# Attention and two MLPs on one core: integer turns and q's second order on ScalarE, the first pair turned on TensorE

## The chip, the cores and the metric

The kernel runs on one core of one Trainium2 chip. The metric is the device time of one execution in microseconds (us); lower is better. The five engines are named as in the profile: PE (TensorE; PEld is its weight load), DVE (VectorE), ACT (ScalarE), POOL (GpSimd) and SP (SyncE, which here only issues DMAs; SPq is its queue).

## What is computed

```python
# q, k, v: (4 batches, 8 heads, 1152 rows, 64), float32
q_pool = q.reshape(B, H, S // 2, 2, D).mean(axis=3)          # 576 query rows
scores = (1 / sqrt(D)) * q_pool @ k.T                         # 576 x 1152 per head
attn = softmax(scores)
x = (attn @ v) -> reshaped to (2304, 512)
h = x @ w_in;    g = h * cos(h);      y = g @ w_out           # 512 -> 2048 -> 512
h2 = y @ w_in2;  g2 = h2 * sigmoid(h2); out = g2 @ w_out2     # 512 -> 2048 -> 512
```

The weights of both MLPs are float64 in memory; the output is (2304, 512) float32. float32 factors are carried as two float16 numbers, a high and a low part, and multiplied on PE as such.

## The kernel before

**Attention.** The heads are handled in 16 pairs (two heads of one batch). A pair has nine tiles of 128 query rows (the ninth holds the last 64 rows of both heads). For each pair `pair_loads` issues the loads of q, k and v on SP's queue, and `pair_prep` prepares them: GpSimd adds the two rows that are averaged, VectorE takes absolute maxima, a small matmul spreads them and three VectorE operations make the scales; then q and k are split into a high and a low float16 part (ScalarE writes the high part, VectorE the low one), and a DMA transpose turns each. q stands twice in the buffer `qn`: once as (high, low) and once as (low, high), so that two matmuls with the same k, which is (high, low), give all cross products. The copy in the other order costs a second ScalarE operation (L509 runs twice) and a VectorE copy (L513), and the transpose of q (L515) has 18 blocks of 128 x 128, as many as that of k (L525).

A tile then goes through a chain: PE makes 128 x 1152 scores (L549, L557) in two PSUM tiles `sp`; VectorE scales them into `sc` and takes the extreme (L568, then `nb` at L573); ScalarE takes the exponential (L576) and the high float16 part (`hl`, L582); GpSimd subtracts to get the low part (L150, three operations); a DMA transpose on SP's queue turns both parts (`hlT`, L589, 18 blocks); PE multiplies with v (L600, L604). PE does the last step of a tile four tiles after its first (`LAG = 4`), and there are four buffers each of `sc`, `hl` and `hlT`.

**First MLP.** While the first batch's four pairs run, the float64 weights are loaded and split (`layer1_weight_steps`). From the second batch on, units of the first MLP are put between the tiles (`share`, `layer1`): nine blocks of 256 tokens, each with 16 slices `f` of the hidden dimension. `g1_unit` makes a slice (12 matmuls, L685) in one half of a PSUM tile `hp` (tag `h`, two buffers); at each odd `f`, `g1_evac` brings two slices to `hk` in SBUF (L701), scaled to turns of h over 2 pi. Four slices make a group, 36 groups in all. `g_cos_begin` rounds the group's turns to whole numbers with the constant MAGIC (L713) and subtracts (L714); `g_cos_end` takes the sine (L720), multiplies by h (L723), makes the high part `gh` (L728) and, on GpSimd, the low part `gl` (L150). The work tile `tt` has two buffers (`NB_TT = 2`), which the finished output `y32` of a block (L749, stored by L752) uses as well. `g2_unit1` is the second product (L740).

**Second MLP.** Behind the last tile of attention the rest of the first MLP runs with the preparation of the second one's weights (`layer2_weight_steps`, L343 to L374), then the second MLP (L685 again, L854).

**Order.** A scheduler orders the instructions of each engine by priorities over a simulated timeline, and waits for a free buffer where a tag has none; `pin` (`tc.keep_in_program_order`) keeps an instruction in the order of the program. So a change in one place shifts the order in others. Each engine and each DMA queue executes its own list in order.

Of the kernel before, what the change touches and what calls it, by code (L numbers as in the profile page):

```python
# [18 lines left out]
DRAM = bass.MemoryType.DRAM  # L19

EXP_MASK = 0x7F800000
MAGIC = 12582912.0
# [5 lines left out]
NB_N, NB_SC, NB_H, NB_T, NB_S = 2, 4, 4, 4, 5  # L28
LOW_HL, LOW_G, LOW_W = 3, 2, 2
X_LAG = 40  # L30
W1_BUFS, WT_BUFS = 3, 3
# [8 lines left out]
NB_HK, NB_TT, NB_G, SIN_N = 2, 2, 2, 2  # L40
# [9 lines left out]
def attention_moe_moe_kernel(ctx, tc, q, k, v, w_in1, w_out1, w_in2, w_out2, out):  # L50
# [3 lines left out]
    nc = tc.nc  # L54
    B, H, S, D = q.shape
# [4 lines left out]
    KC = S // 128  # L60
# [12 lines left out]
    mean = const.tile([128, 128], F32, name="mean")  # L73
    halfpi = const.tile([128, 1], F32, name="halfpi")
    floor3 = const.tile([128, 1], F32, name="floor3")

    def make_consts():
        nc.vector.memset(mean, 2.0**-7)
        nc.vector.memset(halfpi, math.pi / 2)
        nc.vector.memset(floor3, 2.0**-14 - 0.5)  # L80

    GW = 256

# [97 lines left out]
    def layer1_weight_steps(w, srcs, stage, pspool, eng, bufs, wt_bufs, period, offs, first):  # L181
# [71 lines left out]
        for i, x in enumerate(pieces):  # L253
            g = []
            if i < first:
                g.append(piece_steps(*x, lambda ins: ins))
# [179 lines left out]
    def pair_new(at, b, j):  # L436

        P = Pair()  # L440
        P.b, P.j = b, j
        P.on_pool = PREP_POOL if b == 0 else 0
        P.q = at.src.tile([128, 2 * NT + 1, 2, D], F32, tag="stq", name="stq", bufs=1)
        P.k, P.v = (
            [at.src.tile([128, KC, D], F32, tag="stg", name="st" + nm, bufs=NB_S) for i in range(2)] for nm in "kv"
        )
        return P

    def pair_loads(P):
        heads = (P.j, P.j + NP)  # L450
        n = NT * 128 * 2
        for i, h in enumerate(heads):
            nc.sync.dma_start(
                out=P.q[:, i * NT:(i + 1) * NT], in_=q[P.b, h, 0:n, :].rearrange("(p t r) d -> p t r d", t=NT, r=2)
            )
            nc.sync.dma_start(
                out=P.q[i * 64:(i + 1) * 64, 2 * NT], in_=q[P.b, h, n:, :].rearrange("(p r) d -> p r d", r=2)
            )
            yield
        for src, t in ((k, P.k), (v, P.v)):  # L460
            for i, h in enumerate(heads):
                nc.sync.dma_start(out=t[i], in_=src[P.b, h].rearrange("(p c) d -> p c d", c=KC))
                yield

    def split(hi, lo, src, s, on_pool):
        nc.scalar.activation(out=hi, in_=src, func=AF.Copy, scale=s)
        if on_pool:
            nc.scalar.activation(out=src, in_=src, func=AF.Copy, scale=s)
            nc.gpsimd.tensor_tensor(out=lo, in0=src, in1=hi, op=ALU.subtract)
        else:  # L470
            nc.vector.scalar_tensor_tensor(out=lo, in0=src, scalar=s, in1=hi, op0=ALU.mult, op1=ALU.subtract)

    def pair_prep(at, P):
        NQ = 2 * NT + 1
        qs = P.q[:, :, 0, :]
        nc.gpsimd.tensor_tensor(out=qs, in0=qs, in1=P.q[:, :, 1, :], op=ALU.add)
        m = small.tile([128, 5], F32, name="pm", tag="pm")
        for i in range(2):
# [12 lines left out]
        s = small.tile([128, 3], F32, name="ps_", tag="ps_", bufs=3)  # L491
        u = small.tile([128, 3], F32, name="pu_", tag="pu_", bufs=3)
        yield from early(scale_steps(m3, ps_h, (s, u), 12), P_CH)
        P.s = s
        P.su = small.tile([128, 1], F32, name="psu", tag="psu", bufs=3)
        nc.vector.tensor_scalar(
            out=P.su, in0=u[:, 0:1], scalar1=u[:, 1:2], scalar2=-0.125 / math.sqrt(D), op0=ALU.mult, op1=ALU.mult
        )
        P.vt = [None] * 2

        def do_v(i):

            P.vt[i] = vt = at.vt[(2 * (P.b * NP + P.j) + i) % VT_BUFS]
            split(vt[:, :, 0, 0:D], vt[:, :, 1, 0:D], P.v[i], s[:, 2:3], P.on_pool >= 2)


        qn = at.src.tile([128, 2, NQ, 2, D], F16, tag="kn", name="qn", bufs=NB_N)
        for e in range(2):
            nc.scalar.activation(out=qn[:, e, :, e, :], in_=qs, func=AF.Copy, scale=s[:, 0:1])  # L509
        nc.vector.scalar_tensor_tensor(  # L510
            out=qn[:, 0, :, 1, :], in0=qs, scalar=s[:, 0:1], in1=qn[:, 0, :, 0, :], op0=ALU.mult, op1=ALU.subtract
        )
        nc.vector.tensor_copy(qn[:, 1, :, 0, :], qn[:, 0, :, 1, :])  # L513
        qT = at.p.tile([128, 2, NQ, 128], F16, tag="qT", name="qT", bufs=2)
        nc.sync.dma_start_transpose(  # L515
            out=qT.rearrange("p e n k -> p (e n) k"), in_=qn.rearrange("p e n s d -> p (e n s d)")
        )
        P.qT = [qT[:, e] for e in range(2)]
        yield
        kn = at.src.tile([128, 2, KC, 2, D], F16, tag="kn", name="kn", bufs=NB_N)  # L520
# [4 lines left out]
        nc.sync.dma_start_transpose(  # L525
            out=kT.rearrange("p i c k -> p (i c) k"), in_=kn.rearrange("p i c s d -> p (i c s d)")
        )
        P.kT = [kT[:, i].rearrange("p c k -> p (c k)") for i in range(2)]
        yield
        for i in range(2):  # L530
            do_v(i)
            yield

    segs = [(o, min(512, S - o)) for o in range(0, S, 512)]

# [168 lines left out]

    def g_cos_begin(mp, blk):
# [175 lines left out]
    if True:  # L881
# [6 lines left out]
        at = att_pools(att_stack)  # L888
# [161 lines left out]
        for n, (b, j) in enumerate(pairs):  # L1050
# [7 lines left out]
            for o in range(0, len(seq), GT):  # L1058
                G = Pair()
# [211 lines left out]
```

## Time and profile before

| | |
|---|---|
| time, median of 3 runs | 1358.67 us (1353.96 to 1359.51) |
| the profiled execution | 1361.32 us, span of its instructions 1359.5 us |
| busy share of the span | PE 84%, DVE 72%, ACT 64%, POOL 52% |
| mean granted TensorE clock | 0.916 of full speed |
| attention's tiles | first exponential at 31.5 us, last at 816.3 us |
| DMA | 186.29 MB; 465952 of 509597 packets are under 512 bytes |

The profiled execution lies 2.65 us above the median; of its 1361.32 us 1.8 us lie outside the span. In what follows the program falls into five stretches: the start (0 to 30 us, loads and the first pair's preparation), the first batch with the weights of the first MLP (30 to 230 us), attention with the first MLP between (230 to 816 us), the rest of the first MLP with the second one's weights (816 to 1060 us), and the second MLP (1060 us to the end). "Busy" of an engine is an average; an engine waits in order, so a late input delays all that is queued behind it.

### The profile page before, as it was taken

What the parts mean: (1) busy time and instruction counts of PE and PEld (TensorE: products, weight loads), DVE (VectorE), ACT (ScalarE), POOL (GpSimd) and SP (SyncE); (2) the same over time, 40 slices, a digit from 0 to 9 for tenths busy, and PEclk for the clock granted to TensorE, in tenths of its full rate; (3) what the DMA queues carried; (4) which work ended last, traced back from release to release, by engine and by line L of the source; (5) the groups of instructions that cost most, each with busy time, mean ns of one, the idle gap of its engine ahead of it and who ended that gap; (6) DMA issues with size and microseconds to landing.
All of it is one profiled execution on the core that took longest, in us unless ns stands there. A gap on an engine that the chain in (4) does not pass through costs nothing. (4 is left out here: it accounts for less than half of the span.)

```text
span 1359.5 us, 26737 instructions
## 1 busy us (share of the span) xinstructions
PE 1146.0 (84%) x10668; PEld 914.5 (67%) x10668; DVE 981.6 (72%) x1927; ACT 870.0 (64%) x1061; POOL 705.1 (52%) x624
## 2 busy tenths in 40 slices
PE   1564565888988679998898999899999999999998
PEld 0333343666766456675676677788788888888887
DVE  6896978877877777795787795986757755444483
ACT  3896888778777777885788774634546633333352
POOL 1688686688668576875768673533667400000000
PEclk9677676989999888998999999999899999999999
DMA  9999999889799999998999975413344000000001
GB/s 270 210 229 219 224 242 208 152 159 175 139 191 186 195 201 202 191 162 161 164 181 190 197 174 100 128 60 75 82 97 106 32 30 27 9 16 17 17 32 32
DMA packets 509597, 186.29 MB, mean 137 GB/s; under 512 B 465952, under 2 KB 484384, under 8 KB 509472
## 3 DMA queue, kind: packets, MB, share of 16 engines
q1 hardware_dynamic: 509472, 184.59, 65.7%
q8 instruction: 83, 1.36, 0.4%
q14 instruction: 42, 0.34, 0.1%
HBM read 66.58 MB, written 9.44 MB: 56 GB/s over the span
## 5 line engine op out<-in xcount | busy, mean ns | idle before, releaser
L150 POOL TENSOR_TENSOR hl<-sc,hl 128x384 f16<-128x384 f32 x432 | 453.8, 1081 | 145.3 <-ACT hl L582 110.1
L568 DVE TENSOR_SCALAR_CACHE_REDUCE sc<-sp,psu 128x512 f32<-128x512 f32 (+1 forms) x288 | 229.7, 808 | 78.1 <-PE sp L549 66.9
L549 PE MATMUL sp<-kT,qT 128*128 128x512 f16 (+1 forms) x768 | 195.3, 373 | 83.5 <-DVE sc L568 58.7
L685 PEld LDWEIGHTS <-ih 128*128 128x128 f16 x2304 | 226.3, 100 | 45.7 <-issue 13.8
L600 PE MATMUL pv<-vt,hlT 128*128 128x130 f16 (+1 forms) x1440 | 194.6, 236 | 73.8 <-DMA hlT<-hl 68.2
L576 ACT ACTIVATE sc<-sc,nb 128x1152 f32<-128x1152 f32 x144 | 179.4, 1249 | 76.8 <-DVE nb L573 69.7
L600 PEld LDWEIGHTS <-hlT 128*128 128x128 f16 (+1 forms) x1440 | 144.6, 109 | 106.3 <-DMA hlT<-hl 80.9
L685 PE MATMUL h<-ys,ih 128*128 128x256 f16 x1152 | 195.6, 274 | 4.1 <-ACT gs L701 4.1
L685 PE MATMUL h<-xT,ih 128*128 128x256 f16 x1024 | 186.3, 277 | 5.1 <-ACT hk L701 2.1
L604 PE MATMUL pv<-vt,hlT 128*128 128x65 f16 (+1 forms) x1440 | 184.7, 206 | 0.0
L582 ACT ACTIVATE hl<-sc 128x1152 f16<-128x1152 f32 x144 | 165.2, 1154 | 26.2 <-DMA hlT<-hl 20.0
L549 PEld LDWEIGHTS <-qT 128*128 128x128 f16 x768 | 77.1, 109 | 150.9 <-issue 102.5
L740 PE MATMUL y<-gh,oh 128*128 128x256 f16 x576 | 162.8, 283 | 6.8 <-ACT y L749 6.8
L740 PE MATMUL y<-gl,oh 128*128 128x256 f16 x576 | 163.1, 283 | 1.9 <-POOL gl L150 1.9
L740 PE MATMUL y<-gh,ol 128*128 128x256 f16 x576 | 162.6, 282 | 0.0
L854 PEld LDWEIGHTS <-op 128*128 128x128 f16 x1512 | 147.9, 98 | 18.0 <-issue 0.6
L685 PE MATMUL h<-ys,il 128*128 128x256 f16 x576 | 157.7, 274 | 0.0
L604 PEld LDWEIGHTS <-hlT 128*128 128x128 f16 (+1 forms) x1440 | 141.2, 107 | 14.6 <-issue 7.1
L685 PE MATMUL h<-xT,il 128*128 128x256 f16 x512 | 141.8, 277 | 0.0
L150 POOL TENSOR_TENSOR gl<-tt,gh 128x512 f16<-128x512 f32 (+1 forms) x60 | 97.3, 1637 | 79.7 <-DVE gh L728 61.0
L740 PEld LDWEIGHTS <-oh 128*128 128x128 f16 x1152 | 115.4, 102 | 30.8 <-issue 10.3
L685 PEld LDWEIGHTS <-il 128*128 128x128 f16 x1152 | 114.2, 99 | 16.9 <-issue 0.4
(310 smaller groups left out, 1967.6 us busy)
## 6 DMA issues: line engine op xcount, KB each, us to landing
wst<-in_moe_w_in_dram SPq DMA_DIRECT2D x16, 1024.0 KB, 6.1
stk<-in_k_dram SPq DMA_DIRECT2D x32, 288.0 KB, 4.2
stv<-in_v_dram SPq DMA_DIRECT2D x32, 288.0 KB, 4.4
stq<-in_q_dram SPq DMA_DIRECT2D x32, 256.0 KB, 3.1
wst<-in_moe_w_out_dram SPq DMA_DIRECT2D x8, 1024.0 KB, 6.4
wst<-in_moe_w_out_dram SPq DMA_DIRECT2D x16, 512.0 KB, 6.0
ydr<-y SPq DMA_DIRECT2D x9, 512.0 KB, 3.3
y32b<-ydr SPq DMA_DIRECT2D x9, 512.0 KB, 3.3
```

The lines of the kernel that those rows point to most:

```text
L150: last = nc.gpsimd.tensor_tensor(out=lo[:, o:o + w], in0=x[:, o:o + w], in1=hi[:, o:o + w], op=ALU.subtract)
L549: nc.tensor.matmul(sp[:, o - a:o - a + n], P.qT[e][:, t, :], kT[:, o:o + n], start=(e == 0), stop=(e == 1))
L568: nc.vector.tensor_scalar(out=T.sc[:, a:z], in0=sp, scalar1=T.P.su, scalar2=None, op0=ALU.mult, op1=ALU.min, accum_out=mx[:, x:x + 1],)
L576: nc.scalar.activation(out=T.sc, in_=T.sc, func=AF.Exp, scale=-1.0, bias=nb)
L582: nc.scalar.activation(out=hi, in_=T.sc, func=AF.Copy)
L600: nc.tensor.matmul(G.pv[r, T.gi], T.hlT[:, 0, c, r], P.vt[i][:, c], start=(c == 0), stop=(c == KC - 1), skip_group_check=True,)
L604: nc.tensor.matmul(G.pv[r, T.gi, 0], T.hlT[:, 1, c, r], P.vt[i][:, c, 0], start=False, stop=(c == KC - 1), skip_group_check=True,)
L685: nc.tensor.matmul(hp, wt[:, c, f * 128:(f + 1) * 128], xt(c), start=(i == 0), stop=(i == 3 * NC - 1), skip_group_check=True,)
L740: nc.tensor.matmul(blk.y[:, oc, :], wt[:, f, oc * 128:(oc + 1) * 128], gt[:, f % 4, :], start=(f == 0 and e == 0 and oc % 2 == 0), stop=(f ...
L854: nc.tensor.matmul(bank, t[:, e, c, :], wt[:, c, :], start=start, stop=True, skip_group_check=True)
```

## The change

- **First pair (batch 0, pair 0).** Its two k loads are issued by ScalarE's queue. Its q and k are turned by PE transposes (`turn`, 27 blocks) into PSUM and copied to SBUF by ScalarE; no DMA transpose is issued for it. ScalarE's function table is loaded by a dummy operation ahead of the data (`warm`). v's high part and the first weight piece's steps are kept in program order (`pin`).
- **q of every pair.** `qn` holds q once, as (high, low): one ScalarE operation instead of two, no VectorE copy, and a DMA transpose of 9 blocks instead of 18. The second order, (low, high), is made after the transpose by two copies across partition halves (`swap`, 64 x 1152 float16 each): by VectorE for the first pair, by ScalarE for the 15 others, at the end of the pair's preparation. `qn` and `kn` have a buffer each, where both shared two.
- **Integer turns.** The whole number of turns is written by ScalarE at the evacuation, as a second read of the same PSUM tile with an int32 output and a bias of 0.25; VectorE's MAGIC operation is gone and one subtraction is left. The buffer of `tt` is taken at the group's first evacuation instead of after its second.

```diff
     for src, t in ((k, P.k), (v, P.v)):
         for i, h in enumerate(heads):
-            nc.sync.dma_start(out=t[i], in_=src[P.b, h].rearrange("(p c) d -> p c d", c=KC))
+            eng = nc.scalar if P.first and src is k else nc.sync
+            eng.dma_start(out=t[i], in_=src[P.b, h].rearrange("(p c) d -> p c d", c=KC))
...
+    def turn(dst, src):
+        nb = dst.shape[1]
+        for o in range(0, nb, 6):
+            m = min(6, nb - o)
+            pt = ps_h.tile([128, 2, GW], F32, tag="h", name="pt").rearrange("p a n -> p (a n)").bitcast(F16)
+            for i in range(m):
+                nc.tensor.transpose(pt[:, i * 128:(i + 1) * 128], src[:, (o + i) * 128:(o + i + 1) * 128], ident)
+            nc.scalar.activation(
+                out=dst[:, o:o + m].rearrange("p c k -> p (c k)"), in_=pt[:, 0:m * 128], func=AF.Copy
+            )
...
-    qn = at.src.tile([128, 2, NQ, 2, D], F16, tag="kn", name="qn", bufs=NB_N)
-    for e in range(2):
-        nc.scalar.activation(out=qn[:, e, :, e, :], in_=qs, func=AF.Copy, scale=s[:, 0:1])
-    nc.vector.scalar_tensor_tensor(
-        out=qn[:, 0, :, 1, :], in0=qs, scalar=s[:, 0:1], in1=qn[:, 0, :, 0, :], op0=ALU.mult, op1=ALU.subtract
-    )
-    nc.vector.tensor_copy(qn[:, 1, :, 0, :], qn[:, 0, :, 1, :])
+    qn = at.src.tile([128, NQ, 2, D], F16, tag="qn", name="qn", bufs=1)
+    split(qn[:, :, 0, :], qn[:, :, 1, :], qs, s[:, 0:1], False)
     qT = at.p.tile([128, 2, NQ, 128], F16, tag="qT", name="qT", bufs=2)
-    nc.sync.dma_start_transpose(
-        out=qT.rearrange("p e n k -> p (e n) k"), in_=qn.rearrange("p e n s d -> p (e n s d)")
-    )
+    def swap():
+        for x, y in ((slice(0, 64), slice(64, 128)), (slice(64, 128), slice(0, 64))):
+            if P.first:
+                nc.vector.tensor_copy(qT[x, 1], qT[y, 0])
+            else:
+                nc.scalar.activation(out=qT[x, 1], in_=qT[y, 0], func=AF.Copy)
+    if P.first:
+        turn(qT[:, 0], qn.rearrange("p n s d -> p (n s d)"))
+        swap()
+    else:
+        nc.sync.dma_start_transpose(out=qT[:, 0], in_=qn.rearrange("p n s d -> p (n s d)"))
...
     for i in range(2):
         do_v(i)
         yield
+    if not P.first:
+        swap()
+    yield
...
     nc.scalar.activation(
         out=o, in_=blk.hp, func=AF.Copy if first else AF.Silu, scale=blk.c.a[:, g:g + 1]
     )
+    if first:
+        nc.scalar.activation(
+            out=blk.tt.bitcast(I32)[:, (f % 4) - 1:(f % 4) + 1, :], in_=blk.hp, func=AF.Identity,
+            scale=blk.c.a[:, g:g + 1], bias=quarter,
+        )
...
-    G.t = t = mp.p.tile([128, 4, GW], F32, tag="tt", name="tt", bufs=NB_TT)
-    nc.vector.tensor_scalar(out=t, in0=G.hk, scalar1=0.25, scalar2=MAGIC, op0=ALU.add, op1=ALU.add)
-    nc.vector.scalar_tensor_tensor(out=t, in0=t, scalar=MAGIC, in1=G.hk, op0=ALU.subtract, op1=ALU.subtract)
+    G.t = t = blk.tt
+    nc.vector.tensor_tensor(out=t, in0=t.bitcast(I32), in1=G.hk, op=ALU.subtract)
...
     if n == 0:
+        nc.scalar.activation(out=warm, in_=halfpi, func=AF.Copy)
```

On SP's queue, at the beginning of the program, before (`stq`, `stk`, `stv` are the loads of q, k and v, `wst` those of weights; from row 8 on they are the second pair's):

```order
5 L462 DMA stk<-in_k_dram 128x576 x2
6 L462 DMA stv<-in_v_dram 128x576 x2
7 L196 DMA wst<-in_moe_w_in_dram 128x4x512 x3
8 L462 DMA stk<-in_k_dram 128x576
9 L453 DMA stq<-in_q_dram 128x512
10 L515 DMA_TRANSPOSE qT<-qn 128x18x128
11 L525 DMA_TRANSPOSE kT<-kn 128x18x128
12 L456 DMA stq<-in_q_dram 64x128
13 L453 DMA stq<-in_q_dram 128x512
```

and of the change:

```order
5 L471 DMA stv<-in_v_dram 128x576 x2
6 L203 DMA wst<-in_moe_w_in_dram 128x4x512 x3
7 L471 DMA stk<-in_k_dram 128x576
8 L461 DMA stq<-in_q_dram 128x512
9 L464 DMA stq<-in_q_dram 64x128
10 L461 DMA stq<-in_q_dram 128x512
11 L464 DMA stq<-in_q_dram 64x128
12 L471 DMA stk<-in_k_dram 128x576
13 L471 DMA stv<-in_v_dram 128x576 x2
14 L471 DMA stk<-in_k_dram 128x576
15 L621 DMA_TRANSPOSE hlT<-hl 128x18x128 x2
```

The first pair's k loads and both its transposes have left the queue, so that the second pair's loads stand where the transposes stood.

On ScalarE, at the beginning, of the change (before, the list began with the table load for `qn`, then `qn`, `kn` and `vt` two times each, then the weights):

```order
1 L471 DMA stk<-in_k_dram 128x576 x2
2 L999 ACT_TABLE_LOAD
3 L999 ACTIVATE warm<-halfpi 128x1
4 L475 ACTIVATE qn<-stq,ps__171 128x9x64
5 L475 ACTIVATE kn<-stk,ps__171 128x9x64 x2
6 L490 ACTIVATE qT<-pt 128x768
7 L490 ACTIVATE qT<-pt 128x384
8 L490 ACTIVATE kT<-pt 128x768 x3
9 L475 ACTIVATE vt<-stv,ps__171 128x9x64 x2
```

The table load stands ahead of everything that needs data, and five copies out of PSUM stand between `kn` and `vt`.

On ScalarE in the third stretch, around the preparation of a pair (`ps__3251`), before:

```order
223 L701 ACTIVATE hk<-h,ca 128x512
224 L582 ACTIVATE hl<-sc 128x1152
225 L509 ACTIVATE qn<-stq,ps__3251 128x9x64 x2
226 L466 ACTIVATE kn<-stk,ps__3251 128x9x64 x2
227 L576 ACTIVATE sc<-sc,nb 128x1152
228 L466 ACTIVATE vt<-stv,ps__3251 128x9x64
229 L576 ACTIVATE sc<-sc,nb 128x1152
230 L582 ACTIVATE hl<-sc 128x1152 x2
231 L576 ACTIVATE sc<-sc,nb 128x1152
```

and of the change (the same pair, `ps__3299`):

```order
244 L734 ACTIVATE hk<-h,ca 128x512
245 L738 ACTIVATE tt<-h,quarter,ca 128x512
246 L614 ACTIVATE hl<-sc 128x1152
247 L475 ACTIVATE qn<-stq,ps__3299 128x9x64
248 L475 ACTIVATE kn<-stk,ps__3299 128x9x64 x2
249 L608 ACTIVATE sc<-sc,nb 128x1152
250 L475 ACTIVATE vt<-stv,ps__3299 128x9x64
251 L608 ACTIVATE sc<-sc,nb 128x1152
252 L614 ACTIVATE hl<-sc 128x1152
253 L537 ACTIVATE qT<-qT 64x1152 x2
254 L614 ACTIVATE hl<-sc 128x1152
255 L608 ACTIVATE sc<-sc,nb 128x1152
```

Each evacuation is followed by a second one (`tt<-h`), one `qn` is gone, and the two copies of the second order stand five operations behind `kn`, ahead of the high part of a tile.

## Rows read from the trace of the kernel before

**Rows 1.** Windows: PE, PEld, DVE, ACT, POOL busy us; granted clock; DMA share; GB/s.

```profile
30.00:230.00 200.00, 116.84 (x930) 73.01 (x928) 166.38 (x394) 163.55 (x182) 146.96 (x134) 0.69 1.04 227
230.00:816.00 586.00, 505.49 (x5043) 381.63 (x5043) 458.76 (x1002) 451.59 (x537) 417.39 (x383) 0.93 0.94 178
816.00:1060.00 244.00, 225.39 (x1994) 195.04 (x1995) 176.22 (x265) 122.62 (x162) 129.67 (x89) 0.95 0.39 92
1060.00:1360.00 300.00, 294.40 (x2695) 263.06 (x2692) 161.91 (x232) 122.62 (x171) 7.62 (x7) 1.00 0.07 22
```

**Rows 2.** Waits, 30 to 230 us: us in total, times, longest us.

```profile
PE pv L600 <- DMA hlT<-hl: 44.7, 21, 5.0
PE sp L549 <- DVE sc L568: 19.2, 18, 4.0
```

**Rows 3.** Waits, 230 to 816 us.

```profile
POOL hl L150 <- ACT hl L582: 79.9, 31, 7.0
...
PE sp L549 <- DVE sc L568: 38.6, 30, 5.3
...
PE pv L600 <- DMA hlT<-hl: 21.1, 12, 3.4
```

**Rows 4.** Waits of PE, 816 to 1060 us.

```profile
PE h L685 <- ACT hk L701: 3.7, 3, 3.1
```

**Rows 5.** Timeline of the start: start us, us, instruction, idle before and releaser.

```profile
12.35 0.16 DVE L488 TENSOR_REDUCE pm<-pm 128x2 f32<-128x4 f32 x1
...
13.62 1.28 ACT L509 ACT_TABLE_LOAD   x1 [13.62 <-DVE ps__162 L116]
...
14.91 1.44 ACT L509 ACTIVATE qn<-stq,ps__162 128x576 f16<-128x576 f32 x2
15.72 0.82 DVE L510 SCALAR_TENSOR_TENSOR qn<-stq,ps__162,qn 128x576 f16<-128x576 f32 x1 [1.72 <-ACT qn L509]
...
17.14 3.93 SPq L515 DMA_TRANSPOSE qT<-qn  x1
...
21.18 2.76 SPq L525 DMA_TRANSPOSE kT<-kn  x1
...
25.81 2.08 PE L549 MATMUL sp<-kT,qT 128*128 128x512 f16 x6 [12.66 <-DMA kT<-kn]
```

**Rows 6.** The transposes of q on SP's queue (source view): ns min/median/max.

```profile
L515 SPq DMA_TRANSPOSE qT<-qn x16: 2697/2839/3931, 17.1 to 747.9; - x16
```

**Rows 7.** Timeline: two transposes of `hl`, back to back.

```profile
608.30 6.54 SPq L589 DMA_TRANSPOSE hlT<-hl  x2
```

**Rows 8.** Groups by form, 230 to 816 us: busy us, mean ns, idle before.

```profile
L549 PE MATMUL sp<-kT,qT 128*128 128x128 f16 x188 | 27.7, 228 | 0.0
...
L549 PEld LDWEIGHTS <-qT 128*128 128x128 f16 x564 | 53.8, 102 | 86.7 <-issue 59.6 <-DVE sc L568 0.7
...
L582 ACT ACTIVATE hl<-sc 128x1152 f16<-128x1152 f32 x107 | 122.7, 1155 | 13.6 <-DMA hlT<-hl 7.4 <-DMA xT<-xn 5.1
L701 ACT ACTIVATE hk<-h,ca 128x512 f32<-128x512 f32 x47 | 31.5, 675 | 13.4 <-PE h L685 13.4
L713 DVE TENSOR_SCALAR tt<-hk 128x1024 f32<-128x1024 f32 x23 | 21.4, 928 | 5.9 <-ACT hk L701 5.4 <-ACT hl L582 0.4
L513 DVE COPY qn<-qn 128x576 f16<-128x576 f16 x11 | 5.7, 519 | 0.1
```

**Rows 9.** ScalarE's `qn` of the fifth pair (source view): ns, first and last start.

```profile
L509 ACT ACTIVATE qn<-stq,ps__1957 x2: 763/764/764, 202.2 to 202.9; 128x576 f16<-128x576 f32 x2
```

**Rows 10.** Groups by form, 816 to 1060 us.

```profile
L701 ACT ACTIVATE hk<-h,ca 128x512 f32<-128x512 f32 x25 | 17.0, 681 | 12.6 <-PE h L685 12.5
```

**Rows 11.** A cosine group, 505 to 546 us: ScalarE's timeline, then `gl` on GpSimd.

```profile
516.32 0.67 ACT L701 ACTIVATE hk<-h,ca 128x512 f32<-128x512 f32 x1
...
534.88 0.69 ACT L701 ACTIVATE hk<-h,ca 128x512 f32<-128x512 f32 x1 [2.04 <-PE h L685]
...
L150 POOL TENSOR_TENSOR gl<-tt,gh x2: 1157/1652/2146, 541.3 to 543.4; 128x512 f16<-128x512 f32 x2
```

More of the change, by code (lines that the diff above doesn't have):

```diff
@@ L21 @@
 EXP_MASK = 0x7F800000
-MAGIC = 12582912.0
 TINY = 2.0**-50
@@ L27 @@
 PSH = 15.0
-NB_N, NB_SC, NB_H, NB_T, NB_S = 2, 4, 4, 4, 5
+NB_SC, NB_H, NB_T, NB_S = 4, 4, 4, 5
 LOW_HL, LOW_G, LOW_W = 3, 2, 2
@@ L75, in attention_moe_moe_kernel @@
     floor3 = const.tile([128, 1], F32, name="floor3")
+    ident = const.tile([128, 128], F16, name="ident")
+    warm = const.tile([128, 1], F32, name="warm")
+    quarter = const.tile([128, 1], F32, name="quarter")
     def make_consts():
@@ L80, in make_consts @@
         nc.vector.memset(floor3, 2.0**-14 - 0.5)
+        nc.gpsimd.memset(ident, 0.0)
+        nc.gpsimd.affine_select(
+            out=ident, in_=ident, pattern=[[-1, 128]], compare_op=ALU.not_equal, fill=1.0, base=0, channel_multiplier=1
+        )
+        nc.vector.memset(quarter, 0.25)
     GW = 256
@@ L255, in layer1_weight_steps @@
             if i < first:
-                g.append(piece_steps(*x, lambda ins: ins))
+                g.append(piece_steps(*x, pin))
                 for _ in range(2):
@@ L441, in pair_new @@
         P.b, P.j = b, j
+        P.first = (b, j) == (0, 0)
         P.on_pool = PREP_POOL if b == 0 else 0
@@ L461, in pair_loads, with split @@
             for i, h in enumerate(heads):
-                nc.sync.dma_start(out=t[i], in_=src[P.b, h].rearrange("(p c) d -> p c d", c=KC))
+                eng = nc.scalar if P.first and src is k else nc.sync
+                eng.dma_start(out=t[i], in_=src[P.b, h].rearrange("(p c) d -> p c d", c=KC))
                 yield
-    def split(hi, lo, src, s, on_pool):
-        nc.scalar.activation(out=hi, in_=src, func=AF.Copy, scale=s)
+    def split(hi, lo, src, s, on_pool, put=lambda ins: ins):
+        put(nc.scalar.activation(out=hi, in_=src, func=AF.Copy, scale=s))
         if on_pool:
@@ L503, in do_v @@
             P.vt[i] = vt = at.vt[(2 * (P.b * NP + P.j) + i) % VT_BUFS]
-            split(vt[:, :, 0, 0:D], vt[:, :, 1, 0:D], P.v[i], s[:, 2:3], P.on_pool >= 2)
-        qn = at.src.tile([128, 2, NQ, 2, D], F16, tag="kn", name="qn", bufs=NB_N)
-        for e in range(2):
-            nc.scalar.activation(out=qn[:, e, :, e, :], in_=qs, func=AF.Copy, scale=s[:, 0:1])
-        nc.vector.scalar_tensor_tensor(
-            out=qn[:, 0, :, 1, :], in0=qs, scalar=s[:, 0:1], in1=qn[:, 0, :, 0, :], op0=ALU.mult, op1=ALU.subtract
-        )
-        nc.vector.tensor_copy(qn[:, 1, :, 0, :], qn[:, 0, :, 1, :])
-        qT = at.p.tile([128, 2, NQ, 128], F16, tag="qT", name="qT", bufs=2)
-        nc.sync.dma_start_transpose(
-            out=qT.rearrange("p e n k -> p (e n) k"), in_=qn.rearrange("p e n s d -> p (e n s d)")
-        )
+            split(vt[:, :, 0, 0:D], vt[:, :, 1, 0:D], P.v[i], s[:, 2:3], P.on_pool >= 2, *([pin] if P.first else []))
+        qn = at.src.tile([128, NQ, 2, D], F16, tag="qn", name="qn", bufs=1)
+        split(qn[:, :, 0, :], qn[:, :, 1, :], qs, s[:, 0:1], False)
+        qT = at.p.tile([128, 2, NQ, 128], F16, tag="qT", name="qT", bufs=2)
+        def swap():
[9 more added lines that the diff above has]
+            nc.sync.dma_start_transpose(out=qT[:, 0], in_=qn.rearrange("p n s d -> p (n s d)"))
         P.qT = [qT[:, e] for e in range(2)]
         yield
-        kn = at.src.tile([128, 2, KC, 2, D], F16, tag="kn", name="kn", bufs=NB_N)
+        kn = at.src.tile([128, 2, KC, 2, D], F16, tag="kn", name="kn", bufs=1)
         for i in range(2):
@@ L524, in pair_prep @@
         kT = at.p.tile([128, 2, KC, 128], F16, tag="kT", name="kT", bufs=2)
-        nc.sync.dma_start_transpose(
-            out=kT.rearrange("p i c k -> p (i c) k"), in_=kn.rearrange("p i c s d -> p (i c s d)")
-        )
+        if P.first:
+            turn(kT.rearrange("p i c k -> p (i c) k"), kn.rearrange("p i c s d -> p (i c s d)"))
+        else:
+            nc.sync.dma_start_transpose(
+                out=kT.rearrange("p i c k -> p (i c) k"), in_=kn.rearrange("p i c s d -> p (i c s d)")
+            )
         P.kT = [kT[:, i].rearrange("p c k -> p (c k)") for i in range(2)]
@@ L697, in g1_evac @@
                 blk.hk = mp.p.tile([128, 4, GW], F32, tag="hk", name="hk", bufs=NB_HK)
+                blk.tt = mp.p.tile([128, 4, GW], F32, tag="tt", name="tt", bufs=NB_TT)
             o = blk.hk[:, (f % 4) - 1:(f % 4) + 1, :]
@@ L703, in g1_evac @@
         )
+        if first:
+            nc.scalar.activation(
+                out=blk.tt.bitcast(I32)[:, (f % 4) - 1:(f % 4) + 1, :], in_=blk.hp, func=AF.Identity,
+                scale=blk.c.a[:, g:g + 1], bias=quarter,
+            )
     def g_cos_begin(mp, blk):
```

## The prediction, made before the changed kernel ran

> **What bounds the kernel now.** I read the windows of the five stretches first, then the waits of each, then the start's timeline. In the windows [rows 1] the reader is to see three different limits. Behind 1060 us PE works 294.4 of 300 us at full clock, and the change touches nothing there. From 816 to 1060 us PE is busy 225.4 of 244 us, so that at most 18.6 us can be won, and little is waiting to be lost. Ahead of 816 us no engine is full: from 30 to 230 us PE works 117 of 200 us at a granted clock of 0.69, a mix of its two levels, while the DMA engines' share is 1.04; from 230 to 816 us PE works 505 of 586 us, DVE 459, ACT 452, POOL 417, and the DMA share is 0.94. The waits say what that means for PE. In the first batch it waited 21 times, 44.7 us, for a turned tile (`hlT`), with 36 tiles in the batch, and 19.2 us for VectorE to empty the scores [rows 2]. From 230 to 816 us, with 107 tiles [rows 8], it waited 12 times, 21.1 us, for `hlT` and 30 times, 38.6 us, for VectorE; GpSimd waited 31 times for ScalarE's `hl` [rows 3]. So the first batch hangs on the end of the tile's chain, the transposes and their queue; the later batches are a chain in near balance, in which about one tile in nine is late at its end and more than one in four at VectorE.
>
> **The start.** Before, the maxima are ready at 12.35 us, the scales at 13.62 us; then ScalarE loads its table for 1.28 us, and q follows at 14.91 us. Two transposes are issued, at 17.14 us for 3.93 us and at 21.18 us for 2.76 us, and the first score waits for the second until 25.81 us [rows 5]. After: the two k loads no longer stand ahead of those of v on one queue. That brings the last maximum between 0 and 1 us forward, since the bytes stay the same; I take 0.7. The table is loaded, so q begins at 13.62 - 0.7 = 12.9 us; one operation of 0.76 us [rows 9] and the low part, 0.82 us [rows 5], end at 14.5 us. Then 27 PE transposes. Their duration is not in this trace. The nearest rows are a 128 x 128 matmul, 228 ns, with its weight load, 102 ns [rows 8]: at least 0.10 each where loads and matmuls overlap, at most 0.33 where they don't, so 2.8 to 8.9 us; I take 0.2, since the loads do overlap elsewhere, and get 5.4 us. k's split lies beside q's transposes. The first score starts at 14.5 + 5.4 = 19.9 us, 5.9 us sooner (2.4 to 8.5 from the two ends). The copies out of PSUM run beside the transposes but for the last; the first score needs only the first blocks of k.
>
> The Trainium skill speaks to this step and the next. VectorE: DVE Perf Modes, section The three transpose paths, gives 390 ns for a 128 x 128 transpose on TensorE and 1309 ns by DMA, and advises TensorE where PSUM will do. No run here shows the first figure; by it the 27 would last 10.5 us and the start would gain 0.8 us. The second disagrees with the trace: two transposes of 18 blocks back to back took 6.54 us [rows 7], 0.18 us a block.
>
> **Nine blocks fewer per transpose.** q's transposes held SP's queue for 2.84 us, median, for 18 blocks [rows 6], and 0.18 us a block follows from the pair of `hl` [rows 7]. Half is 1.4 to 1.6 us; I take 1.42 for each of 15 pairs. Preparation of the second to fifth pair falls before 230 us (the fifth at 202.2 us [rows 9]), that of 11 pairs after. In the first batch, where the DMA share is 1.04, I count nearly all of 4 x 1.42: -5. For the 11 pairs the whole is 15.6 us, and by PE's late tiles (12 of 107) it would be 1.7; between them I take -6, since a DMA share of 0.94 says that little of the queue's time is free.
>
> **More work on ScalarE.** A second evacuation costs what the first does, 0.675 us [rows 8], for 47 of them 31.7 us from 230 to 816 us, and 25 x 0.68 = 17.0 us from 816 to 1060 us [rows 10]. The second order of q costs two operations of 1152 elements per partition; with the nearest row, of that length, 1.155 us [rows 8], and less one `qn` of 0.76 us [rows 9], a pair gives 1.55 us more: 17.0 us for 11 pairs, 6.2 us for the four. So ScalarE goes from 452 to 500 of 586 us. How much reaches PE? An instruction put into an ordered queue delays what follows until a gap takes it up. PE saw one tile in nine late, GpSimd 31 of 107 late because of ScalarE [rows 3]: shares of 0.11 and 0.29. I take 0.2: 48.7 x 0.2 = +9.7 us, and 6.2 x 0.2 = +1 in the first batch. The copies also wait for the transposed q, with the exponential or high part of the next tile queued behind them, for which GpSimd and at last PE wait. They stand only five or so operations behind `kn`; 1 us each, at the same share, is +2. That wait isn't in the trace of before; from nothing to +10.
>
> **Less on VectorE.** L713 goes, 23 x 0.93 = 21.4 us, and L513, 11 x 0.52 = 5.7 us [rows 8]; the subtraction that is left I count as what it was. VectorE made PE wait for 30 of 107 tiles [rows 3]: 27.1 x 0.28 = -7.6 us, with nothing and -15 as ends.
>
> **The work tile held longer.** `tt` is now taken at the group's first evacuation. In the group shown, that is at 516.32 us instead of behind 534.88 us, while GpSimd ends with the tile before at about 545 us [rows 11]; with two buffers and `y32` in them, an evacuation can wait for GpSimd, with PE's `hp` behind it. Ahead of 816 us the scheduler has tiles to put in between, and PE's own waits for evacuation are few. From 816 to 1060 us, where they were 3.7 us in all [rows 4], I take +3 for this and the second evacuation together, from 0 to the 17 us that ScalarE gains in work.
>
> **At no cost.** The dummy operation and the k loads stand on ScalarE where it idled until 13.62 us [rows 5]. The separate buffers of `qn` and `kn` have a pair's time to come free. The identity is written on GpSimd ahead of q's addition.
>
> **The sum.** -5.9 - 5 - 6 + 9.7 + 1 + 2 - 7.6 + 3 = -8.8 us. Against the profiled execution, 1361.3 us, that is 1352.5; it lay 2.65 us above the median of the runs, 1358.67, from which I count: 1350 us, 0.65% faster. What a measurement of this kernel can tell from no change is about 0.5%, 6.8 us. Own range of this case, with the terms' ends: 1342 to 1356.
>
> **Rivals.**
> *ScalarE becomes the bound.* Place: the third stretch. All terms without ScalarE's are -5.9 - 5 - 6 - 7.6 + 2 = -22.5; its extra work is 48.7 + 6.2 + 17.0 = 71.9 us. The change breaks even when 0.31 of that reaches PE's path and is slower by 0.5% from 0.41 on. At one half: -22.5 + 36 + 2 for longer waits of the copies = +15.5, 1374 us. For it: 85% busy in order, two visits of each tile; against it: POOL's waits for `hl` ended in PE's lateness in one tile of nine only. The Trainium skill has the same warning: ScalarE: Activation LUTs, Rules for kernel authors, wants adds and multiplies on VectorE, up to about three times faster per element in 16 bits. The trace bears that out little here: VectorE's copy took 0.52 us for 576 elements [rows 8], about 1.0 for 1152, against ScalarE's 1.16. Chance 0.20.
> *The queue is the bound throughout.* Then all of 15.6 us comes back in the third stretch and gaps on ScalarE take up more of its work (a share of 0.1): -5.9 - 5 - 15.6 - 7.6 + 7.2 + 2 = -24.9, 1334 us. For it the DMA share, against it the 12 waits of 107. Chance 0.16.
> *The gain of the start is taken back.* The first batch must move the same weights and loads at a DMA share of 1.04; if these bytes set its end, the sooner first score only waits longer. Then start and batch together give about -4, the third stretch cancels (-6 - 7.6 + 9.7 + 2), the fourth costs 3: -3, 1356 us. Chance 0.26.
> The forecast has the remaining 0.38.
>
> **Range and chances.** 1333 to 1368 leaves out the worse half of the first rival and the better part of the second, not quite 2 in 10. Faster: 0.16 + 0.34 of the forecast + 0.02 = 0.52. Same: 0.04 + 0.22 + 0.02 = 0.28. Slower: 0.18 + 0.02 = 0.20.
>
> **What would show it.** The first score near 20 us with 27 PE transposes ahead of it within some 5 us; SP's issue of q's transposes near 1.4 us; the first batch's last exponential some 10 us sooner, with fewer waits of PE for `hlT` in it; ACT at about 500 us and DVE at about 430 us in what is now 230 to 816 us; PE's waits for VectorE down, its waits for `hlT` there not up by more than half; waits of ScalarE for the transposed q of about 1 us a pair; from the last tile to the end about as long as before, 543 us, give or take 5. The prediction is wrong if PE's waits for `hlT` double behind 230 us, if the second evacuation holds PE in the fourth stretch, or if the new order of the instructions, which shifts on every engine, makes or mends other waits larger than these terms.

## The result and the profile after

| | before | after |
|---|---|---|
| time, median | 1356.96 us of 4 runs (1353.96 to 1359.51) | 1338.82 us of 4 runs (1337.11 to 1340.45) |
| ratio, 95% interval | | 0.9867, 0.984 to 0.9894 |
| profiled execution: span, mean granted clock | 1359.5 us, 0.916 | 1335.2 us, 0.919 |
| first exponential | 31.5 us | 24.1 us |
| fifth pair's first exponential | 230.2 us | 235.7 us |
| last exponential | 816.3 us | 792.8 us |
| from it to the end | 543.2 us | 542.4 us |

The change made the kernel 1.3% faster. The time lies in the range predicted, 11 us under the forecast. The two profiled executions lie 24.3 us apart, the medians 18.1. By the exponentials the 24.3 us divide so: 7.4 won until the first one, 12.9 lost from there to the fifth pair, 29.0 won from there to the last, 0.8 won behind it. The forecast had spoken of a gain in the first batch and of a third stretch in balance.

The start, timeline of the changed kernel (start us, us, instruction, idle before and releaser):

```profile
9.78 0.16 DVE L509 TENSOR_REDUCE pm<-pm 128x2 f32<-128x4 f32 x1
...
11.06 0.77 ACT L475 ACTIVATE qn<-stq,ps__171 128x576 f16<-128x576 f32 x1 [7.91 <-DVE ps__171 L123]
...
12.74 1.14 PE L489 MATMUL pt<-ident,qn 128*128 128x128 f16 x9 [2.17 <-DVE qn L480]
...
14.46 1.44 PE L489 MATMUL pt<-ident,kn 128*128 128x128 f16 x12 [0.58 <-ACT qT L490]
...
16.16 1.01 PE L581 MATMUL sp<-kT,qT 128*128 128x512 f16 x2 [0.26 <-ACT kT L490]
...
16.96 0.85 PE L489 MATMUL pt<-ident,kn 128*128 128x128 f16 x6
```

Beside [rows 5] everything is sooner: the last maximum by 2.57 us, `qn` by 3.85, the first score, 16.16 against 25.81, by 9.65.

Waits of the changed kernel, 30 to 230 us (us in total, times, longest):

```profile
PE sp L581 <- DVE sc L600: 37.7, 24, 9.1
...
PE pv L632 <- DMA hlT<-hl: 32.8, 15, 5.7
POOL stq L497 <- DMA stq<-in_q_dram: 25.0, 3, 11.1
```

and one line of the same view of the kernel before:

```profile
POOL stq L476 <- DMA stq<-in_q_dram: 9.9, 3, 3.5
```

PE's wait for turned tiles fell from 44.7 to 32.8 us, and its wait for VectorE rose from 19.2 to 37.7 [rows 2]. GpSimd's three waits for q's load grew from 9.9 to 25.0 us. The same view of the changed kernel's third stretch, 236 to 793 us:

```profile
POOL hl L157 <- ACT hl L614: 56.4, 26, 7.1
...
PE sp L581 <- DVE sc L600: 37.6, 32, 5.5
...
ACT sc L608 <- DVE nb L605: 19.8, 14, 3.6
PE pv L632 <- DMA hlT<-hl: 19.3, 14, 3.4
...
ACT qT L537 <- DMA qT<-qn: 4.3, 3, 2.1
```

What PE waited for is nearly as before [rows 3]. ScalarE's waits ahead of an exponential for VectorE's `nb` shrank; the kernel before has there, from 230 to 816 us:

```profile
ACT sc L576 <- DVE nb L573: 56.5, 26, 8.6
```

The new operations of the changed kernel, groups by form, 236 to 793 us (busy us, mean ns, idle before), and q's transposes on SP's queue (source view: ns min/median/max):

```profile
L738 ACT ACTIVATE tt<-h,quarter,ca 128x512 int32<-128x512 f32 x46 | 35.0, 768 | 2.8 <-POOL gl L157 2.8
L734 ACT ACTIVATE hk<-h,ca 128x512 f32<-128x512 f32 x47 | 31.7, 673 | 8.3 <-PE h L717 8.2
...
L537 ACT ACTIVATE qT<-qT 64x1152 f16<-64x1152 f16 x22 | 25.6, 1162 | 4.7 <-DMA qT<-qn 4.3
```

```profile
L751 DVE TENSOR_TENSOR tt<-tt,hk 128x1024 f32<-128x1024 int32 x23 | 33.4, 1451 | 7.0 <-ACT tt L738 7.0
```

```profile
L543 SPq DMA_TRANSPOSE qT<-qn x15: 1279/1315/2017, 46.3 to 721.6; - x15
```

The windows by its own exponentials (columns as in [rows 1]; from the fifth pair to the last exponential, then to the end):

```profile
235.70:792.80 557.10, 487.06 (x4958) 372.54 (x4956) 434.61 (x955) 492.87 (x591) 422.31 (x381) 0.95 0.93 179
792.80:1335.20 542.40, 519.03 (x4753) 459.99 (x4750) 329.33 (x484) 264.55 (x362) 139.82 (x96) 0.99 0.22 55
```

VectorE works 24 us less than in [rows 1], ScalarE 41 us more, and yet the stretch is 29 us shorter. From 793 to 1060 us PE waits for the second evacuation (`tt`) once; the waits for `gs` belong to the second MLP:

```profile
PE h L717 <- ACT gs L734: 8.0, 5, 3.4
PE y L777 <- ACT y L786: 5.1, 3, 2.5
PE h L717 <- ACT tt L738: 3.2, 1, 3.2
```

### The profile page after: what moved, and what is told of

Same layout as the page of the kernel before. It is cut to its first block, busy times and chain, and to the rows that moved or that the text cites. A ratio compares the mean times of both kernels' runs of the same rounds, so it can differ in the third digit from the quotient of the medians.

```text
span 1335.2 us, 26781 instructions
## 1 busy us (share of the span) xinstructions
PE 1136.0 (85%) x10695; PEld 915.5 (69%) x10695; DVE 958.4 (72%) x1878; ACT 940.4 (70%) x1151; POOL 713.0 (53%) x626
## 5 line engine op out<-in xcount | busy, mean ns | idle before, releaser
L157 POOL TENSOR_TENSOR hl<-sc,hl 128x384 f16<-128x384 f32 x432 | 460.7, 1099 | 122.0 <-ACT hl L614 99.5
L581 PE MATMUL sp<-kT,qT 128*128 128x512 f16 (+1 forms) x768 | 190.9, 365 | 82.1 <-DVE sc L600 81.1
L632 PEld LDWEIGHTS <-hlT 128*128 128x128 f16 (+1 forms) x1440 | 148.0, 111 | 92.5 <-DMA hlT<-hl 65.6
L777 PE MATMUL y<-gh,oh 128*128 128x256 f16 x576 | 159.6, 277 | 5.9 <-ACT y L786 5.7
L777 PE MATMUL y<-gh,ol 128*128 128x256 f16 x576 | 159.4, 277 | 0.0
L777 PE MATMUL y<-gl,oh 128*128 128x256 f16 x576 | 159.4, 277 | 0.0
L636 PEld LDWEIGHTS <-hlT 128*128 128x128 f16 (+1 forms) x1440 | 144.1, 109 | 12.9 <-issue 4.9
L157 POOL TENSOR_TENSOR gl<-tt,gh 128x512 f16<-128x512 f32 (+1 forms) x60 | 102.2, 1720 | 68.3 <-DVE gh L765 53.5
```

What stands on the lines that cost most here:

```text
L157: last = nc.gpsimd.tensor_tensor(out=lo[:, o:o + w], in0=x[:, o:o + w], in1=hi[:, o:o + w], op=ALU.subtract)
L581: nc.tensor.matmul(sp[:, o - a:o - a + n], P.qT[e][:, t, :], kT[:, o:o + n], start=(e == 0), stop=(e == 1))
L632: nc.tensor.matmul(G.pv[r, T.gi], T.hlT[:, 0, c, r], P.vt[i][:, c], start=(c == 0), stop=(c == KC - 1), skip_group_check=True,)
L636: nc.tensor.matmul(G.pv[r, T.gi, 0], T.hlT[:, 1, c, r], P.vt[i][:, c, 0], start=False, stop=(c == KC - 1), skip_group_check=True,)
L777: nc.tensor.matmul(blk.y[:, oc, :], wt[:, f, oc * 128:(oc + 1) * 128], gt[:, f % 4, :], start=(f == 0 and e == 0 and oc % 2 == 0), stop=(f ...
```

## The experiments

The first theory, A: the change's work decides, since less stands on SP's queue and on VectorE. Its rival, B: the edits also give every engine a new order, and that alone moves the time. A third, C: loads of the next pair come late, and VectorE, whose maxima for that pair stand ahead of a tile's scores, stops with everything behind it.

All twelve in one table, with both kernels (medians; before was 1358.59 us beside the first four, 1357.70 beside the next four, 1356.92 beside the last four). "Fifth pair" is its first exponential, "third" from there to the last exponential, "end" from there to the end, all of the profiled execution; "`nb`" is ScalarE's waits for VectorE ahead of an exponential in the third stretch, from the view of the waits. The stretches are those of one execution each; executions of one kernel lie up to 10 us apart.

| kernel | us | ratio, 95% | first exp. | fifth pair | third | end | `nb` |
|---|---|---|---|---|---|---|---|
| before | 1356.96 | | 31.5 | 230.2 | 586.1 | 543.2 | 56.5 |
| after | 1338.82 | 0.984 to 0.9894 | 24.1 | 235.7 | 557.1 | 542.4 | 19.8 |
| s1_start | 1349.04 | 0.9909 to 0.9956 | 24.4 | 230.3 | 580.8 | 540.5 | 67.8 |
| s2_q | 1340.38 | 0.9847 to 0.989 | 28.6 | 232.5 | 564.9 | 541.3 | 23.5 |
| s3_turns | 1342.70 | 0.9865 to 0.9904 | 29.6 | 225.4 | 577.3 | 536.0 | 33.7 |
| s4_order | 1346.40 | 0.9892 to 0.9928 | 29.6 | 231.0 | 572.2 | 542.6 | 29.9 |
| n1_yield | 1335.95 | 0.9827 to 0.9875 | 30.7 | 227.6 | 570.2 | 540.5 | 39.8 |
| n3_yield2 | 1342.00 | 0.9868 to 0.9913 | 30.4 | 228.7 | 571.8 | 542.1 | 49.2 |
| a1_noyield | 1343.80 | 0.9877 to 0.9922 | 23.9 | 236.7 | 564.9 | 541.5 | 19.1 |
| a2_nopins | 1336.57 | 0.9822 to 0.9869 | 31.3 | 235.0 | 561.7 | 539.3 | 12.6 |
| l3_no_start | 1324.29 | 0.9739 to 0.9785 | 28.6 | 229.8 | 557.5 | 538.1 | 16.9 |
| l1_no_turns | 1342.74 | 0.9878 to 0.9927 | 24.7 | 234.9 | 567.3 | 538.9 | 25.1 |
| x1_after_loads | 1346.02 | 0.9899 to 0.9946 | 24.1 | 235.6 | 566.3 | 543.5 | 18.3 |
| x2_before_loads | 1346.17 | 0.9906 to 0.9942 | 29.7 | 229.5 | 574.7 | 543.9 | 45.4 |

**One part at a time, and the order alone.** s1_start has the first pair's edits, with the change's pins, on the kernel before; its identity stands in a buffer of `hl`:

```diff
+                eng = nc.scalar if P.first and src is k else nc.sync
...
+            turn(qT[:, 0], qn.rearrange("p n s d -> p (n s d)"))
...
+            turn(kT.rearrange("p i c k -> p (i c) k"), kn.rearrange("p i c s d -> p (i c s d)"))
...
+                nc.scalar.activation(out=warm, in_=halfpi, func=AF.Copy)
```

> Only the edits of the first pair (k loaded by ScalarE's queue, table loaded at once, q and k turned on PE, second order by VectorE); all other pairs and the turns as before. Theory A (less work decides): the first score comes 9 us sooner, the first batch takes it back, so the time is 1353 to 1359 us, and the stretch from the fifth pair's first exponential to the last one keeps its 586 us within 4, since no work in it has changed. Theory B (the order of the instructions decides): that stretch moves by more than 6 us either way though its work is the same, and the time with it.

s2_q has q once, the transpose of nine blocks and ScalarE's copies, for all sixteen pairs. It also has the change's extra `yield` behind them, which by itself gives another order (s4_order and n1_yield below):

```diff
-        nc.sync.dma_start_transpose(
-            out=qT.rearrange("p e n k -> p (e n) k"), in_=qn.rearrange("p e n s d -> p (e n s d)")
-        )
+        nc.sync.dma_start_transpose(out=qT[:, 0], in_=qn.rearrange("p n s d -> p (n s d)"))
...
+        swap()
```

> Only q held once, with a transpose of 9 blocks and the second order by two ScalarE copies, for all 16 pairs (the first one too, by DMA). Theory A: the halved transposes and the missing VectorE copies give 6 to 12 us, 1345 to 1351 us, in the third stretch. Theory B: the time moves by an amount that has nothing to do with the work, and the gain of the parts does not add up to the 18 us of all of them.

s3_turns has the integer turns alone:

```diff
+            nc.scalar.activation(
+                out=blk.tt.bitcast(I32)[:, (f % 4) - 1:(f % 4) + 1, :], in_=blk.hp, func=AF.Identity,
...
-        nc.vector.tensor_scalar(out=t, in0=G.hk, scalar1=0.25, scalar2=MAGIC, op0=ALU.add, op1=ALU.add)
```

> Only the integer turns by ScalarE. Theory A: VectorE's 21 us less in the third stretch give 6 to 14 us there, 1343 to 1351 us, more than ScalarE's extra costs. The losing rival of the prediction (ScalarE fills up): 1360 us or more. Theory B: no rule; the third stretch moves in jumps of single long waits, not a little in every pair.

s4_order changes no work; it has only the change's extra `yield` in the pair's preparation and its pins:

```diff
-                g.append(piece_steps(*x, lambda ins: ins))
+                g.append(piece_steps(*x, pin))
...
             do_v(i)
             yield
+        yield
```

> Control: none of the work is changed. Only what the change does to the order besides: one more step at the end of a pair's preparation, v's high part of the first pair and the first weight piece's steps kept in program order. Theory A: 1357 us within 3. Theory B: it moves by 6 us or more, either way, as far as the three parts do.

Each part alone won 10, 18 and 16 us, 44 us together where the whole change won 18, and the order alone won 12 us without any change of work. So what a part wins against the kernel before can't be put down to the part. s4_order moved as B said. s2_q and s3_turns were faster than A's ranges, 1345 to 1351 and 1343 to 1351 us, and s1_start's third stretch moved by 5.3 us, between the 4 of A and the 6 of B.

**More orders of the same work.** n1_yield has one extra `yield` at the end of the preparation on the kernel before, n3_yield2 two:

```diff
             do_v(i)
             yield
+        yield
```

> A second control on the kernel before: one more step at the end of a pair's preparation and nothing else, no work changed. If the arrangement of the kernel before is an unlucky one (theory B), this is faster than it too, 1340 to 1354 us, and the pair that lasted 64.5 us (the thirteenth) lasts some 50. If the first control was a lucky one, this is 1355 us or more.

> A third control on the kernel before: two more steps at the end of a pair's preparation, no work changed. Theory B: again a time of its own between 1340 and 1360 us; the spread of the three controls is the size of what order alone does. Theory A: 1357 us within 3.

a1_noyield takes the `yield` out of the changed kernel, a2_nopins its pins:

```diff
             swap()
-        yield
```

> The changed kernel without the extra step at the end of a pair's preparation: all of the changed work, another order. If less work is worth some 10 us whatever the order, it stays 1330 to 1345 us, below the controls of the kernel before by about that. If the change's time was luck of order, it is anywhere up to 1355 us.

```diff
-                g.append(piece_steps(*x, pin))
+                g.append(piece_steps(*x, lambda ins: ins))
```

> The changed kernel with v's high part of the first pair and the first weight piece's steps left to the scheduler: the same work, another order in the first batch. Less work decides: 1330 to 1345 us. Luck of order: up to 1355 us. The first batch, which lasted 211.6 us from its first exponential against 198.7 before, moves if the pins are what lengthened it, to 200 to 205 us.

One extra step that does no work, 1335.95 us, is as good as the whole change. The work of before ran in five orders (with x2_before_loads below) at 1335.95, 1342.00, 1346.17, 1346.40 and 1357: the kernel before is the unlucky one, and the other four, the rearrangements, have a mean of 1342.6. The work of after ran in four (with x1_after_loads): 1336.57, 1338.82, 1343.80, 1346.02, mean 1341.3. With a standard deviation of 4 to 5 us in each set, the difference, 1.3 us, can't be told from none. With the kernel before counted in, its work has a mean of 1345.5 us, and the difference, 4.2 us, is about its standard error. a2_nopins begins its exponentials at 31.3 us, 7 us later than after, and loses nothing by it.

**Without the first pair's edits, and without the turns.** Two runs take parts away: q and turns together, without what belongs to the first pair, and the changed kernel without the turns:

```diff
-            eng = nc.scalar if P.first and src is k else nc.sync
...
-            turn(qT[:, 0], qn.rearrange("p n s d -> p (n s d)"))
...
-                nc.scalar.activation(out=warm, in_=halfpi, func=AF.Copy)
```

> q once with its halved transposes and ScalarE's copies for all sixteen pairs, and the integer turns, without the edits of the first pair (k on SP's queue, no transposes on TensorE, no early table, no pins). No work is left out. The theory that the first pair's edits are given back in the first batch and that the rest is worth 10 us in the third stretch: first exponential near 29, the fifth pair's near 229 us (changed kernel: 235.7), third stretch near 561, time near 1332 (1328 to 1338). The theory that the order decides and the work is worth little: anywhere among the controls, 1336 to 1346, with the third stretch no shorter than their 570 to 572.

```diff
-                out=blk.tt.bitcast(I32)[:, (f % 4) - 1:(f % 4) + 1, :], in_=blk.hp, func=AF.Identity,
...
+        nc.vector.tensor_scalar(out=t, in0=G.hk, scalar1=0.25, scalar2=MAGIC, op0=ALU.add, op1=ALU.add)
```

> The changed kernel with the turns as before (two VectorE passes, no second copy out of PSUM by ScalarE). No work is left out. If the integer turns relieve VectorE in the third stretch, that stretch becomes 4 to 8 us longer than the changed kernel's 557 (and the two other runs with all the work near 561 to 565), with a time of 1342 to 1347. If ScalarE's second copy costs as much as VectorE gains, as the prediction summed it (+9.7 against -7.6), the time stays at 1337 to 1340 or falls. If the order decides, neither: a time of 1334 to 1346 whichever way.

l3_no_start, 1324.29 us, beats both kernels and every other run. Its windows (as above, and up to the second pair's first exponential) and waits (30 to 230 us):

```profile
0.00:75.60 75.60, 32.66 (x210) 19.80 (x211) 58.82 (x136) 53.34 (x57) 36.49 (x45) 0.80 0.92 236
...
229.80:787.30 557.50, 489.33 (x4972) 372.96 (x4970) 437.05 (x957) 491.89 (x588) 417.37 (x380) 0.95 0.93 179
787.30:1325.40 538.10, 517.01 (x4752) 459.25 (x4750) 328.51 (x486) 263.38 (x361) 140.78 (x95) 0.99 0.22 55
```

```profile
PE sp L551 <- DVE sc L570: 45.8, 22, 6.4
...
PE pv L602 <- DMA hlT<-hl: 17.5, 10, 3.8
```

The third stretch is that of the changed kernel, 557.5 us; the fifth pair starts 5.9 us sooner, and the end is 4.3 us shorter. The expectation was 1332; the 8 us below it are within what orders differ by above, and this work ran in one order only. l1_no_turns moved to the side that a relief of VectorE by the turns asks for: its third stretch is 567.3 us, 10 us above the changed kernel's where 4 to 8 were expected, but only 1.0 above the longest stretch with the turns (x1_after_loads, 566.3). Its time is 1.4 us above the mean of the orders with the turns and can't be told from one more order.

**Loads ahead of their turn.** The same line on the changed kernel (x1) and on the kernel before (x2):

```diff
-                yield from slowly(pair_loads(P[n + 1]), LD_PACE[late])
+                yield from early(slowly(pair_loads(P[n + 1]), LD_PACE[late]), 150)
```

> The changed kernel with the loads of the next pair issued ahead of their turn (a priority that puts them early in the order). No work changes. The theory that late loads make VectorE and GpSimd stand still in the middle of a pair's chunks: the waits of GpSimd's q addition for q's load (25.0 us in three waits before the fifth pair) and of VectorE's maxima for k's and q's loads nearly vanish, the fifth pair starts at 229 or earlier (changed kernel: 235.7), and the time falls to 1328 to 1334. If these waits are only where a wait for something else shows, the waits move, the fifth pair stays at 233 to 237, and the time stays at 1335 to 1345.

> The kernel before with the loads of the next pair issued ahead of their turn, no work changed. The theory that late loads made the 13th pair 64.5 us long: no pair over 52 us, waits for loads nearly gone, time 1335 to 1345 as the three controls without changed work. The theory that any new order would do as well, by chance: a time in the same stretch, but with long pairs elsewhere and waits for loads no smaller than before. If loads are not what stalled it and order matters little: 1354 to 1360.

The theory of the late loads isn't borne out. In x1 GpSimd's waits for q's loads up to the fifth pair went from 25.0 us to

```profile
POOL stq L497 <- DMA stq<-in_q_dram: 4.9, 1, 4.9
```

and the fifth pair still starts at 235.6 us, the time is 7 us longer. The edit did not take away VectorE's own waits for k's loads, 12.4 us from 30 to 230 us against 10.2; but l3_no_start has 11.4 there and an early fifth pair. In x2 the 13th pair, the longest of the kernel before, went from 64.5 to 57.1 us, but the waits for the loads of q and k in the third stretch are no shorter, 17.5 and 21.2 us against 9.7 and 22.5, so that x2 is one more order and no test. And the fastest run, l3_no_start, waits for them there twice as long as the kernel before:

```profile
POOL stq L478 <- DMA stq<-in_q_dram: 32.1, 8, 9.0
DVE pm L129 <- DMA stk<-in_k_dram: 30.9, 11, 4.9
```

## Why the prediction came out as it did

The side and the range were right by luck, for a reason that the sum did not hold: the kernel before's own order costs about as much as the whole change won, since any of four rearrangements without a change of work is 11 to 22 us faster. The prediction names this only in its last sentence, as something that could make it wrong, with no term and no chance. That is the step that failed: the waits of [rows 2, 3] were read as limits of the work, and are in part those of one order. What makes that order slow is shown in part: its 13th pair takes 64.5 us, that of the rearrangements 49 to 57. The wait behind that stays open; s3_turns has the same long pair, 65.3 us, with other waits in it. The terms came out so.

**The start, -5.9: mis-sized, then lost.** The first score came 9.65 us sooner, beyond the end of 8.5 us. The last maximum came 2.57 us sooner, not 0.7: k landed 3.18 us sooner on its own queue (VectorE's first maximum of k at 4.67 us, before at 7.85). A transpose took 0.127 us (nine in 1.14), not 0.2, and six of the 27 came only behind the first score. The Trainium skill, VectorE: DVE Perf Modes, section The three transpose paths, has 390 ns for one on TensorE; the trace disagrees where they stand back to back. But the second pair's first exponential comes at 76.9 us, before at 74.6; in the six kernels with the first pair's edits it comes at 73.9 to 76.9 us, in the eight others at 71.6 to 76.5. The windows up to there, of the changed kernel

```profile
0.00:76.90 76.90, 34.73 (x239) 21.20 (x240) 60.27 (x134) 55.08 (x60) 32.85 (x45) 0.73 0.82 215
```

and of the kernel before:

```profile
0.00:74.60 74.60, 30.10 (x183) 16.91 (x184) 57.78 (x131) 47.40 (x51) 33.21 (x42) 0.83 0.97 240
```

VectorE works 57.8 us of 74.6 before and 60.3 of 76.9 after; it stands still for 16.8 and 16.6 us. In s1_start, a2_nopins and l3_no_start it is 60.3 of 75.9, 58.8 of 73.8 and 58.8 of 75.6, wherever the first exponential was. Before, it had done weights' work while the first scores were late (timeline of the kernel before):

```profile
20.06 1.22 DVE L214 TENSOR_SCALAR_CACHE_REDUCE wt<-wt 128x1024 f32<-128x1024 f32 x1
...
21.39 1.22 DVE L218 SCALAR_TENSOR_TENSOR wt<-wt,wst 128x1024 int32<-128x1024 int32 x1
```

So the rival "the gain of the start is taken back" came true there, but not by its mechanism: the DMA share did not stay full, it fell from 0.97 to 0.82. VectorE's nearly equal work and idle time point to VectorE, but no run relieved it there, and the granted clock fell as well, from 0.83 to 0.73; the cause is argued, not shown.

**The first batch, -5 and +1: no gain, and a loss beside the first pair's edits.** The halved transposes took 1.315 us each on the queue (1.42 predicted). PE's waits for `hlT` fell to 32.8 us, in l3_no_start to 17.5; its waits for VectorE rose by as much or more, to 37.7 and 45.8 us, and the fifth pair came no sooner, 229.8 us in l3_no_start. "The first batch hangs on the end of the tile's chain" was the wrong reading: with less of the one wait there was more of the other, and no time was won. How the waits divide hangs on the order too; a2_nopins, with the same halved transposes, has from 30 to 230 us nearly those of the kernel before:

```profile
PE pv L632 <- DMA hlT<-hl: 39.4, 19, 5.5
...
PE sp L581 <- DVE sc L600: 19.5, 22, 3.8
```

With both the first pair's edits and q once the fifth pair comes at 234.9 to 236.7 us in five kernels, without this pair of edits at 225.4 to 232.5 in nine; from the second pair's first exponential on the five need 158 to 161 us for it, the nine 154 to 156. Why stays open: late loads of q are in four of the five, but not in x1_after_loads.

**The third stretch, -6 + 9.7 + 2 - 7.6: too little.** Where the work is unchanged it lasts 570.2 to 574.7 us in the four rearrangements, 586.1 in before; with q and turns 557.1 to 566.3 in five kernels, mean 561.5: 11 us less, where -1.9 was summed. The two ranges do not touch, and that is the part of the change that the runs show to be worth something, though in four of the five the later fifth pair takes more than half of it back. The nearest rearrangement, n1_yield, has this window and, from its waits, this line:

```profile
227.60:797.80 570.20, 495.94 (x4989) 375.05 (x4990) 456.39 (x1000) 450.07 (x534) 419.97 (x382) 0.94 0.97 183
```

```profile
ACT sc L577 <- DVE nb L574: 39.8, 25, 5.2
```

ScalarE's more work, 48.7 us in the prediction and 41 in the windows, was to cost 9.7. But the exponential had waited for VectorE, 29.9 to 49.2 us in the rearrangements, and waits 12.6 to 19.8 with the change. All of ScalarE's waits for VectorE in this stretch, summed over the view, are 86 to 107 us in the rearrangements, 65 and 67 with q once and no turns (s2_q, l1_no_turns), 76 with the turns alone, and 31 to 44 in the five kernels with both. No order of the old work comes near that: the new work went into time in which ScalarE had waited. Whether VectorE's results came sooner or ScalarE came to them later is not separated; q once takes little from VectorE (453.6 us busy in s2_q, 455 to 463 in the rearrangements) and yet takes a quarter or more of these waits. A share of lateness counted for each engine by itself misses that a tile can be late on one because of the other. q once brings the larger part of the shorter stretch (564.9 and 567.3 us without turns). What the turns add, some 5 us on top of it, is not clear of the spread, and alone (577.3) they can't be judged: that stretch holds the long 13th pair, as the 586.1 of the kernel before does. Single prices were near: the second evacuation 0.768 us (0.675), VectorE's remaining subtraction 1.451 (as before, 1.445), ScalarE's copies 1.162 (1.155). Their wait for the transposed q was 4.3 us for 11 pairs, where 1 us each had been taken.

**The fourth stretch, +3: about nothing.** From the last exponential to the end it is 542.4 us against 543.2, and 539.3 to 543.5 in the orders of the changed work against 540.5 to 543.9 in those of the old. PE waited once, 3.2 us, for the second evacuation.

**The rivals.** ScalarE did not become the bound at 492.9 of 557.1 us. "The queue is the bound throughout" gave a time near the measured one, 1334 us, but PE waited for `hlT` as long as before, 19.3 us against 21.1 [rows 3], in a stretch 29 us shorter.

## What to carry to other kernels

Where a scheduler or priorities set the order, run a control or two that change the order and no work before a gain of 1% is put down to an edit; here five orders of the same work span 21 us. Value an edit against the mean of such orders and stretch by stretch. A head start at the beginning has to be looked for in the next stretch: here the first score came 9.65 us sooner and the second pair no sooner, VectorE having nearly the same work and idle time up to there, and leaving the first pair's edits out gave the fastest kernel, 1324.29 us.

## What the runs showed of the hardware

- Transposes of 128 x 128 float16 on PE, back to back: 0.12 to 0.14 us each (nine in 1.14 us, twelve in 1.44, six in 0.85).
- A copy between partition halves on ScalarE, 64 x 1152 float16, took 1.162 us, as long as an operation of 128 x 1152 from float32, 1.155 us [rows 8]: the same length along a partition, on half as many partitions.
- A second read of a PSUM tile by ScalarE with a bias tile and an int32 output took 0.768 us, the first, without bias and to float32, 0.673.
- VectorE's subtraction of 128 x 1024 took 1.451 us with one operand in int32, and 1.445 us before, from float32 with a constant subtracted as well.
